# Input tiles spread over all partitions and loaded at once, at the head of a fused Fourier and two-layer kernel

## The chip, the core and the metric

The kernel runs on one core of a Trainium2 chip. The metric is device time in microseconds (us). The five engines are TensorE (PE, matmuls; its weight loads are PEld), VectorE (DVE), ScalarE (ACT), GpSimd (POOL) and SyncE (SP). DMAs are issued from queues of SP, ACT or POOL and are carried by 16 DMA engines. SBUF is the on-chip memory of 128 partitions, PSUM holds the results of matmuls.

## What is computed

The input x has two batches of 3008 tokens with 256 values. A Fourier stage mixes tokens, two dense layers follow:

```
X = np.fft.rfft(x, axis=1)
Yr = Xr @ w_r - Xi @ w_i + b_r
Yi = Xr @ w_i + Xi @ w_r + b_i
Y = soft threshold of Yr, Yi by 0.01
x = np.fft.irfft(Y, n=3008, axis=1)
h = x @ w_in;  x = (h * clip(h + 3, 0, 6) / 6) @ w_out
x = (silu(x @ w_gate) * (x @ w_val)) @ w_out2
```

## The kernel before

The transform of length 3008 = 47 x 64 is done in two stages. The first one (`pre(n)`, lines L239 to L254) takes a tile of x: 94 rows (two sets of 47, padded to QP = 96) on the partitions and 1024 columns. It multiplies it with the table `fwd1_sb` (two matmuls of 512 columns, four records in the trace, at L245), evicts the halves on ACT (L248) and DVE (L250) into a buffer `bs` of a ring of four, and writes it to a DRAM scratch `Bd` from ACT's queue (L252). That DMA is kept back in `out_b` and issued in the next tile's `pre`, after its copies. Each batch has NT = 8 tiles; tiles 0 to 7 are the first batch, 8 to 15 the second.

The second stage works on groups Q of four frequencies. `load_q` loads a table `m` (L270) and `z`, the transposed view of Bd (L279); it needs all eight writes of the batch. `s2` (S in the order below, L287 to L294) does the second transform, in two halves, with evictions on ACT and DVE and a split into a high and a low part, `xh` and `xl`. `ln` (L) mixes with the complex weights `linh`, `linl` in three passes at L113, L114 and L115, thresholds on DVE, and `ia` (A, L333) begins the way back. After that units of the dense layers follow, to the end of the kernel.

The loads: `load_x(n)` (L213) puts tile n into one of four buffers of the ring `xal`/`xah`, which are needed later by the dense layer under the same names. Three tiles are loaded ahead, then `pre(n)` loads tile n + 3, and waits on SP until the buffer is free. The mixing weights (`lin_st`), the bias and `inv2_sb`, a table for the last transform, are loaded from POOL's queue, in `prepare` (L228), and POOL splits the weights into high and low parts. Three matmuls on zeros (L225) run before the first tile arrives.

The order of the work is written out by hand in the list `seq` (L366): tile 0, `prepare`, tiles 1 to 7, the load of the first group, tiles 8 to 10, S(0); then, for each group, L, A, S of the next group, and two of the tiles that are left (`rest`) while there are any. `pre_conv` also steps the conversion of the dense layer's weights (`conv1`: loads `st` at L151, small steps on ACT and DVE) from tile 9 on. DMA semaphores are eight and are used in turn, so that a DMA can also wait for an earlier one that raised the same semaphore.

Of the kernel before, what the change touches and what calls it, by code (L numbers as in the profile page):

```python
# [24 lines left out]
QP = 96  # L25
# [15 lines left out]
def dft_tables():  # L41


    tp = 2 * np.pi
    n1 = np.arange(N1)
    f = np.zeros((N1, NG, 2))
    for g in range(NG):
        a = tp * ((n1 * g) % N1) / N1
        f[:, g, 0], f[:, g, 1] = np.cos(a), -np.sin(a) * (g > 0)
    fwd1 = np.zeros((2, N1, NG, 2, 2))  # L50
    for q in range(2):
        fwd1[q, :, :, q, :] = f
    fwd1 = np.pad(fwd1.reshape(QN, GW), ((0, QP - QN), (0, 0)))
    fwd2 = np.zeros((NG, 2, 2, NJ, 2, K2))
    inv1 = np.zeros((NG, 2, K2, 2, 2, NJ))
    for g in range(NG):
        k = g + N1 * np.arange(K2)
        own = np.ones(K2) if g else (np.arange(K2) <= K2 // 2) * 1.0
        edge = (k == 0) | (k == SEQ // 2)
        sg = np.where(k > SEQ // 2, -1.0, 1.0)  # L60
        w = np.where(edge, 1.0, 2.0) / SEQ
        for q in range(2):
            a = tp * (np.outer(2 * np.arange(NJ) + q, k) % SEQ) / SEQ
            c, sn = np.cos(a) * own, np.where(edge, 0.0, np.sin(a)) * own
            ci = np.where(edge, 0.0, c)
            fwd2[g, q, 0, :, 0], fwd2[g, q, 0, :, 1] = c, -sn * sg
            inv1[g, 0, :, q, 0], inv1[g, 1, :, q, 0] = (w * c).T, -(w * sn * sg).T
            if g:
                fwd2[g, q, 1, :, 0], fwd2[g, q, 1, :, 1] = sn, c * sg
                inv1[g, 0, :, q, 1], inv1[g, 1, :, q, 1] = (w * sn).T, (w * ci * sg).T  # L70
    fwd2 = fwd2.reshape(NG, 128, 128).transpose(1, 0, 2).reshape(128, NG * 128)
    inv1 = inv1.reshape(NG, 128, 128).transpose(1, 0, 2).reshape(128, NG * 128)
    out = {"fwd1": fwd1, "inv2": fwd1.T, "fwd2": fwd2, "inv1": inv1}
    return {n: np.ascontiguousarray(v, dtype=np.float32) for n, v in out.items()}


# [1 line left out]
def fourier_moe_kernel(ctx: ExitStack, tc: tile.TileContext, x, lin, bias, w1, w2, fwd1, inv2, fwd2,  # L78
# [39 lines left out]
        nc.vector.tensor_tensor(out=o, in0=full, in1=hi.bitcast(F32), op=ALU.subtract)  # L118

    misc = pool(ctx, "misc", "left")  # L120
    fwd1_sb = misc.tile([QP, GW], F32, name="fwd1_sb")
    inv2_sb = misc.tile([GW, QP], F32, name="inv2_sb")

    three = misc.tile([128, 32], F32, name="three")[:, :1]
# [87 lines left out]

    def load_x(n):  # L213
        b, i = divmod(n, NT)
        if b < NB:
            xt[n] = xs_p.tile([128, 4 * DIM], F32, tag="xah" if n % 2 else "xal", name=f"x{b}_{i}", bufs=2)
            nc.sync.dma_start(xt[n][:QP], x[b][:, i * 4 * DIM : (i + 1) * 4 * DIM])

    nc.sync.dma_start(fwd1_sb, fwd1)
    for n in range(3):  # L220
        load_x(n)

    p = psf[0]([128, 512], "p0")
    for n in range(3):
        nc.tensor.matmul(p, zeros[:, :128], zeros, start=True, stop=True)  # L225
    conv1 = pieces(w1p, "w1", w1, KF1, 2, W1)

    def prepare():  # L228
        lin_st = ap_.tile([128, 2, 2, DIM], F32, tag="z", name="lin_st", bufs=3)
        nc.gpsimd.dma_start(lin_st, lin)  # L230
        nc.gpsimd.dma_start(bias_sb, bias)
        nc.gpsimd.dma_start(inv2_sb, inv2)
        for dh in range(2):
            for k in range(2):
                hi, lo, st = linh[:, dh, k], linl[:, dh, k], lin_st[:, dh, k]
                nc.gpsimd.tensor_copy(hi, st)
                nc.gpsimd.tensor_tensor(out=lo, in0=st, in1=hi.bitcast(F32), op=ALU.subtract)

    def pre(n):  # L239
        b, i = divmod(n, NT)  # L240
        load_x(n + 3)
        bs = ring4(f"bs{b}_{i}")
        for h in range(2):
            p = psf[0]([GW, 512], f"p1_{b}_{i}_{h}")
            nc.tensor.matmul(p, fwd1_sb, xt[n][:QP, h * 512 : (h + 1) * 512], start=True, stop=True)  # L245
            o = bs[:GW, h * 512 : (h + 1) * 512]
            if h == 0:
                nc.scalar.copy(o, p)  # L248
            else:
                nc.vector.tensor_copy(o, p)  # L250
        sent()
        out_b.append(lambda: nc.scalar.dma_start(Bd[b][:, i * 4 * DIM : (i + 1) * 4 * DIM], bs[:GW]))  # L252
        if i == NT - 1:
            sent()  # L254
# [554 lines left out]
```

## Time and profile before

| what | us |
|---|---|
| median of 3 runs (1246.06 to 1247.27) | 1246.06 |
| profiled execution | 1247.67 |
| its span | 1245.9 |
| PE busy | 1228.3 |
| DVE busy | 809.8 |
| ACT busy | 679.7 |

The span is the time from the first to the last instruction in the profiled execution, and times below count from its start. A chain of waits is followed back from the last instruction; each piece of it is either work or the landing of a DMA that released the next piece. The time of a DMA is told from its issue to its landing.

### The profile page before, as it was taken

To read this page: it belongs to the slowest core of one execution; us is meant where nothing else is said; L and a number is where in the kernel's file an instruction comes from. 1 tells how busy PE (TensorE), PEld (TensorE's weight loads), DVE (VectorE), ACT (ScalarE), POOL (GpSimd) and SP (SyncE) were. 2 spreads that over 40 slices of the span, in tenths; PEclk is the share of its full clock that TensorE was granted. 3 is DMA by queue.
4 is the path that set the end of the run, shared out by engine and by line. 5 is a ranking of instruction groups with operands and counts; after the bars stand their busy time and mean duration, and the time that the engine had idled before them with its cause. 6 is when DMAs were issued, how large, how long until landed. Compare 5 with 4: busy or idle time off the path is not lost.

```text
span 1245.9 us, 15942 instructions
## 1 busy us (share of the span) xinstructions
PE 1228.3 (99%) x5914; PEld 1034.2 (83%) x5914; DVE 809.8 (65%) x1424; ACT 679.7 (55%) x1216; POOL 6.3 (1%) x15
## 2 busy tenths in 40 slices
PE   7899999999999999999999999999999999999998
PEld 2799987888888888888899888888888888888997
DVE  2587665666666666666656577676676676676665
ACT  2455544555555555555555566656656555656554
POOL 2000000000000000000000000000000000000000
PEclk9899999999999999999999999999999999999999
DMA  9976323033122122132032244554644644544551
GB/s 305 279 258 191 102 77 105 28 100 103 64 91 93 59 70 93 64 100 91 39 105 91 72 175 170 203 182 152 220 158 170 235 153 152 216 157 168 203 186 72
DMA packets 50285, 172.84 MB, mean 139 GB/s; under 512 B 4752, under 2 KB 18160, under 8 KB 39456
## 3 DMA queue, kind: packets, MB, share of 16 engines
q1 hardware_dynamic: 41856, 158.55, 37.4%
q10 hardware_dynamic: 8128, 12.58, 2.8%
q8 instruction: 46, 0.75, 0.2%
q0 software_dynamic: 224, 0.69, 0.2%
q14 instruction: 31, 0.25, 0.1%
HBM read 132.75 MB, written 39.06 MB: 138 GB/s over the span
## 4 chain that ended last, share of the span: by engine, by line
PE 96%; DMA 2%; DVE 0%; ACT 0%; issue 0%; SPq 0%; ACTq 0%; DVEq 0%
PE acc L114 12%; PE acc L115 12%; PE acc L113 12%; PE ph L113 7%; PE ph L115 7%; PE ph L114 7%; PE P L662 5%; PE P L663 5%; PE P L664 5%; PE Tb L663 3%; PE Tb L662 3%; PE Tb L664 3%; PE p L419 3%; PE p L113 2%; PE p L115 2%; PE p L114 2%
## 5 line engine op out<-in xcount | busy, mean ns | idle before, releaser
L434 DVE SCALAR_TENSOR_TENSOR r<-r,ph 128x512 f32<-128x512 f32 (+1 forms) x192 | 129.7, 676 | 83.3 <-ACT r L433 82.8
L118 DVE TENSOR_TENSOR gl<-r,gh 128x512 fp32r<-128x512 f32 (+1 forms) x192 | 130.1, 678 | 82.4 <-ACT gh L452 81.0
L433 ACT ACTIVATE r<-ph,three 128x512 f32<-128x512 f32 (+1 forms) x192 | 130.2, 678 | 96.1 <-PE ph L115 80.6
L452 ACT CAST gh<-r 128x512 fp32r<-128x512 f32 (+1 forms) x192 | 117.3, 611 | 84.4 <-DVE r L434 82.7
L113 PE MATMUL ph<-xah,w1l 128*128 128x512 f32 (+1 forms) x384 | 152.1, 396 | 0.0
L113 PE MATMUL acc<-gh,w1l 128*128 128x512 f32 (+1 forms) x384 | 148.3, 386 | 1.5 <-ACT gh L452 1.5
L114 PE MATMUL acc<-gl,w1h 128*128 128x512 f32 (+1 forms) x384 | 148.2, 386 | 0.2 <-DVE gl L118 0.2
L115 PE MATMUL ph<-xah,w1h 128*128 128x512 f32 (+1 forms) x384 | 148.2, 386 | 0.0
L114 PE MATMUL ph<-xal,w1h 128*128 128x512 f32 (+1 forms) x384 | 148.1, 386 | 0.0
L115 PE MATMUL acc<-gh,w1h 128*128 128x512 f32 (+1 forms) x384 | 148.1, 386 | 0.0
L118 DVE TENSOR_TENSOR gl<-s,gh 128x512 fp32r<-128x512 f32 (+1 forms) x144 | 97.3, 676 | 49.8 <-ACT gh L686 49.7
L662 PE MATMUL P<-xo,slot 128*128 128x512 f32 (+1 forms) x288 | 111.3, 386 | 1.7 <-DVE g L732 0.8
L114 PE MATMUL acc<-gl,slot 128*128 128x512 f32 (+1 forms) x288 | 111.1, 386 | 0.3 <-DVE gl L118 0.2
L113 PE MATMUL acc<-gh,slot 128*128 128x512 f32 (+1 forms) x288 | 111.0, 385 | 0.0
L664 PE MATMUL P<-xo,slot 128*128 128x512 f32 (+1 forms) x288 | 110.9, 385 | 0.0
L115 PE MATMUL acc<-gh,slot 128*128 128x512 f32 (+1 forms) x288 | 110.9, 385 | 0.0
L663 PE MATMUL P<-xo,slot 128*128 128x512 f32 (+1 forms) x288 | 110.9, 385 | 0.0
L728 ACT ACTIVATE s<-g 128x512 f32<-128x512 f32 (+1 forms) x72 | 44.9, 623 | 93.7 <-DVE g L726 93.7
L686 ACT CAST gh<-s 128x512 fp32r<-128x512 f32 (+1 forms) x144 | 88.1, 612 | 1.5 <-DVE s L745 1.2
L113 PEld LDWEIGHTS acc<-gh,w1l 128*128 128x128 f32 x384 | 72.1, 188 | 15.4 <-ACT gh L452 1.9
L114 PEld LDWEIGHTS acc<-gl,w1h 128*128 128x128 f32 x384 | 72.1, 188 | 14.6 <-DVE gl L118 0.9
L115 PEld LDWEIGHTS ph<-xah,w1h 128*128 128x128 f32 x384 | 72.1, 188 | 14.0
(94 smaller groups left out, 2258.7 us busy)
## 6 DMA issues: line engine op xcount, KB each, us to landing
slot<-Wd SPq DMA_DIRECT2D x72, 1152.0 KB, 5.1
st<-in_w SPq DMA_DIRECT2D x68, 256.0 KB, 3.8
Wd<-slot SPq DMA_DIRECT2D x12, 1152.0 KB, 4.7
x<-in_x SPq DMA_DIRECT2D x16, 384.0 KB, 6.5
Bd<-bs ACTq DMA_DIRECT2D x16, 384.0 KB, 5.9
z<-Bd SPq DMA_DIRECT2D x12, 512.0 KB, 6.1
Cd<-cs ACTq DMA_DIRECT2D x12, 512.0 KB, 3.5
Xd<-x SPq DMA_DIRECT2D x20, 256.0 KB, 2.1
```

What stands on the lines that cost most here:

```text
L113: nc.tensor.matmul(o, wl, xh, start=start, stop=False)
L114: nc.tensor.matmul(o, wh, xl, start=False, stop=False)
L115: nc.tensor.matmul(o, wh, xh, start=False, stop=stop)
L118: nc.vector.tensor_tensor(out=o, in0=full, in1=hi.bitcast(F32), op=ALU.subtract)
L433: nc.scalar.activation(r[:, :n], p[:, :n], AF.Relu, bias=three)
L434: nc.vector.scalar_tensor_tensor(out=r[:, :n], in0=r[:, :n], scalar=6.0, in1=p[:, :n], op0=ALU.min, op1=ALU.mult)
L452: nc.scalar.copy(hi[:, :n], g[:, :n])
L662: nc.tensor.matmul(o, wl, x[:, 0, :n], start=start, stop=False, skip_group_check=not start)
L663: nc.tensor.matmul(o, wh, x[:, 1, :n], start=False, stop=False, skip_group_check=not start)
L664: nc.tensor.matmul(o, wh, x[:, 0, :n], start=False, stop=True, skip_group_check=not start)
L686: nc.scalar.copy(hi[:, :nb], t[:, :nb])
L728: nc.scalar.activation(s0[:, :n], h, AF.Silu)
```

## The change

- `fwd1_sb` becomes 128 x 192. Its first 96 columns are the old table in the first 96 rows. In the second 96 columns the first 64 rows of the table lie on the even partitions, the last 32 on partitions 1, 5, 9 and so on, and the other partitions are zero.
- A tile of x can come in two forms: as before on partitions 0 to 95 (tiles 0, 1, 8, 9, 12, 13), or spread in the same pattern over all 128 partitions, by two DMAs (the others). For the spread form six buffers are filled with zeros once, three by DVE and three by POOL, and their matmuls contract over 128 partitions.
- The input lies in DRAM tile by tile now; it was row by row.
- The first batch has eight buffers: the four of the ring and four that the attention stage uses later (`xl`, `xh`). All eight tiles are issued at the start, with `lin_st` and the bias, now from SP's queue, between tiles 4 and 5. Tiles 8 to 11 are issued in `pre(1)` to `pre(4)`, 12 to 15 in `pre(9)` to `pre(12)`.
- Two matmuls on zeros instead of three. `prepare` is only POOL's splitting, and `inv2_sb` is loaded at group NQ of the loop, from SP.
- Four tiles of the second batch (8 to 11) run before S(0), and tile 12 between S(0) and the first L. Three are left for the loop instead of five. The conversion is stepped from tile 11 on.

```diff
-    out = {"fwd1": fwd1, "inv2": fwd1.T, "fwd2": fwd2, "inv1": inv1}
+    both = np.zeros((128, 2 * GW))
+    both[:QP, :GW] = fwd1
+    both[::2, GW:], both[1::4, GW:] = fwd1[:64], fwd1[64:]
...
-        if b < NB:
-            xt[n] = xs_p.tile([128, 4 * DIM], F32, tag="xah" if n % 2 else "xal", name=f"x{b}_{i}", bufs=2)
-            nc.sync.dma_start(xt[n][:QP], x[b][:, i * 4 * DIM : (i + 1) * 4 * DIM])
+        t = xt[n] = room[n if n < NT else n % 4][:, : 4 * DIM]
+        if n % 4 < 2 and not 4 <= n < NT:
+            nc.sync.dma_start(t[:QP], x[b, i])
+        else:
+            nc.sync.dma_start(t[::2], x[b, i, :64])
+            nc.sync.dma_start(t[1::4], x[b, i, 64:])
...
+        if n > 1:
+            (nc.gpsimd if n % 2 else nc.vector).memset(t[:, : 4 * DIM], 0.0)
+    for n in range(5):
         load_x(n)
+    lin_st = ap_.tile([128, 2, 2, DIM], F32, tag="z", name="lin_st", bufs=3)
+    nc.sync.dma_start(lin_st, lin)
+    nc.sync.dma_start(bias_sb, bias)
+    for n in range(5, NT):
+        load_x(n)
...
-    for n in range(3):
+    for n in range(2):
         nc.tensor.matmul(p, zeros[:, :128], zeros, start=True, stop=True)
...
-        load_x(n + 3)
+        if 1 <= n <= 4:
+            load_x(n + 7)
+        elif 9 <= n <= 12:
+            load_x(n + 3)
...
-        if n > NT:
+        if n > NT + 2:
             conv1.step()
...
-    seq = P[:1] + [prepare] + P[1:NT] + [lambda: load_q(0, 0)] + P[NT : NT + 3] + S(0)
-    rest = P[NT + 3 :]
+    seq = [prepare] + P[:NT] + [lambda: load_q(0, 0)] + P[NT : NT + 4] + S(0) + P[NT + 4 : NT + 5]
+    rest = P[NT + 5 :]
...
-            seq += [lambda: load_ct(blocks[0])]
+            seq += [lambda: nc.sync.dma_start(inv2_sb, inv2), lambda: load_ct(blocks[0])]
```

SP's queue at the head of the program, before: the loads of tiles 4 to 7 of batch one and tiles 0 to 2 of batch two (`x0_` and `x1_`), then the table and z of the first group. `DMAHW` are the DMA semaphores, `PE` is a wait for matmuls.

```order
L217 DMA x0_4_171<-in_x 96x1024 [waits DMAHW1_49,PE_49]
L217 DMA x0_5_181<-in_x 96x1024 [waits DMAHW2_49,PE_49]
L217 DMA x0_6_191<-in_x 96x1024 [waits DMAHW3_49,DMAHW0_49,PE_49]
L217 DMA x0_7_201<-in_x 96x1024 [waits DMAHW4_49,PE_49]
L217 DMA x1_0_211<-in_x 96x1024 [waits DMAHW5_49,PE_49]
L217 DMA x1_1_221<-in_x 96x1024 [waits DMAHW7_49,DMAHW6_49,PE_49]
L217 DMA x1_2_231<-in_x 96x1024 [waits DMAHW0_49,PE_49]
L270 DMA m0_242<-in_fwd2 128x512 [waits DMAHW2_49]
```

The same queue now, from tile 4 to tile 7 of batch one (`room4` to `room7`, two DMAs each).

```order
L222 DMA room4_114<-in_x 64x1024 [waits DMAHW0_49,DVE_49]
L223 DMA room4_114<-in_x 32x1024 [waits DMAHW2_49]
L238 DMA lin_st_130<-in_lin 128x1024 [waits DMAHW3_49]
L239 DMA bias_sb_106<-in_bias 128x256 [waits DMAHW5_49]
L222 DMA room5_116<-in_x 64x1024 [waits DMAHW6_49,Pool_49]
L223 DMA room5_116<-in_x 32x1024 [waits DMAHW0_49]
L222 DMA room6_118<-in_x 64x1024 [waits DMAHW1_49,DVE_49]
L223 DMA room6_118<-in_x 32x1024 [waits DMAHW2_49]
L222 DMA room7_120<-in_x 64x1024 [waits DMAHW3_49,Pool_49]
L223 DMA room7_120<-in_x 32x1024 [waits DMAHW5_49]
```

No wait for PE is left there, but semaphores are. ACT's rows of now tell which DMA two of them belong to: the copy into `bs0_4`, which has the buffer of `bs0_0`, waits for the first write of Bd by DMAHW6, and the copy into `bs0_5` for the second by DMAHW1. The loads of `room5` and `room6` wait for the same two.

```order
L274 DMA Bd0_60<-bs0_0_182 96x1024 [waits DVE_49,Activation_49]
L270 COPY bs0_2_199<-p1_0_2_0_200 96x512 [waits PE_49]
L274 DMA Bd0_60<-bs0_1_190 96x1024 [waits DMAHW1_49,DVE_49,Activation_49]
L270 COPY bs0_3_209<-p1_0_3_0_210 96x512 [waits PE_49]
L274 DMA Bd0_60<-bs0_2_199 96x1024 [waits DMAHW4_49,DVE_49,Activation_49]
L270 COPY bs0_4_219<-p1_0_4_0_220 96x512 [waits DMAHW6_49,PE_49]
L274 DMA Bd0_60<-bs0_3_209 96x1024 [waits DMAHW7_49,DVE_49,Activation_49]
L270 COPY bs0_5_227<-p1_0_5_0_228 96x512 [waits DMAHW1_49,PE_49]
```

The writes follow the copies of the next tile, as they did. On PE around S(0), before: the last tile of batch two ahead of it (`p1_1_2`), S(0) itself (`p2_0_0`), and the first mixing matmuls (`p3_0_0`).

```order
L245 MATMUL p1_1_2_0_270<-x1_2_231,fwd1_sb_82 96x512 [waits DMAHW0_49,Activation_49]
L245 MATMUL p1_1_2_1_273<-x1_2_231,fwd1_sb_82 96x512 [waits DVE_49]
L287 MATMUL p2_0_0_0_285<-m0_242,z0_0_244 128x128 [waits DMAHW6_49,DMAHW2_49,DVE_49]
L287 MATMUL p2_0_0_0_285<-m0_242,z0_0_244 128x128 x3
L287 MATMUL p2_0_0_1_294<-m0_242,z0_0_244 128x128 [waits Activation_49]
L287 MATMUL p2_0_0_1_294<-m0_242,z0_0_244 128x128 x3
L113 MATMUL p3_0_0_0_309<-linh_104,xl_0_0_284 128x256 [waits DVE_49,Pool_49]
```

PE at the same place now.

```order
L267 MATMUL p1_1_3_0_284<-room3_112,fwd1_sb_82 96x512 [waits DMAHW7_49,DMAHW5_49,Activation_49]
L267 MATMUL p1_1_3_1_287<-room3_112,fwd1_sb_82 96x512 [waits DVE_49]
L309 MATMUL p2_0_0_0_299<-m0_252,z0_0_254 128x128 [waits DMAHW2_49,DMAHW0_49,Activation_49]
L309 MATMUL p2_0_0_0_299<-m0_252,z0_0_254 128x128 x3
L309 MATMUL p2_0_0_1_308<-m0_252,z0_0_254 128x128 [waits DVE_49]
L309 MATMUL p2_0_0_1_308<-m0_252,z0_0_254 128x128 x3
L265 MATMUL p1_1_4_0_320<-room0_108,fwd1_sb_82 96x512 [waits DMAHW3_49,Activation_49]
L265 MATMUL p1_1_4_1_323<-room0_108,fwd1_sb_82 96x512 [waits DVE_49]
L116 MATMUL p3_0_0_0_335<-linh_104,xl_0_0_298 128x256 [waits DVE_49,Pool_49]
```

Tile 11 (`p1_1_3`) has moved ahead of S(0), and tile 12 (`p1_1_4`) between it and the mixing.

## Rows read from the trace of the kernel before

**Rows 1.** The page, engines: busy us, share of the span, instructions.

```profile
PE 1228.3 (99%) x5914; PEld 1034.2 (83%) x5914; DVE 809.8 (65%) x1424; ACT 679.7 (55%) x1216; POOL 6.3 (1%) x15
```

**Rows 2.** Chain of waits, 0 to 45 us: start, us, what.

```profile
1.66 7.00 DMA x<-in_x
...
22.30 6.03 DMA Bd<-bs
...
28.45 5.74 DMA z<-Bd
...
34.33 2.06 PE p L287 x8
...
40.09 0.36 PE p L113
...
42.56 1.72 PE p L245 x4
44.28 1.79 PE p L287 x16
```

**Rows 3.** Timeline, PE, first 30 us: start, us, instruction, [idle before <- releaser].

```profile
1.48 4.80 PE L225 MATMUL p<-zeros 128*128 128x512 f32 x6 [1.48 <-DVE zeros L127]
...
6.12 1.88 PE L245 MATMUL p<-x,fwd_sb 96*96 96x512 f32 x4
...
8.70 12.75 PE L245 MATMUL p<-x,fwd_sb 96*96 96x512 f32 x28 [0.70 <-DMA x<-in_x]
...
24.23 3.75 PE L245 MATMUL p<-x,fwd_sb 96*96 96x512 f32 x8 [0.61 <-DMA x<-in_x]
```

**Rows 4.** DMA view, 2 to 11 us, then 11 to 28: packets, MB, share.

```profile
DMA packets 757, 2.44 MB, mean 271 GB/s; under 512 B 158, under 2 KB 158, under 8 KB 757
q1 hardware_dynamic: 533, 1.75, 71.9%
...
DMA packets 1827, 6.17 MB, mean 363 GB/s; under 512 B 257, under 2 KB 257, under 8 KB 1827
q1 hardware_dynamic: 890, 2.86, 51.6%
q10 hardware_dynamic: 937, 3.31, 50.6%
```

**Rows 5.** DMA view, issues at 1.20, 9.90, 22.30, 28.45, 28.95, 34.21: us to landing.

```profile
x<-in_x SPq DMA_DIRECT2D x1, 384.0 KB, 4.0
...
Bd<-bs ACTq DMA_DIRECT2D x1, 384.0 KB, 4.1
...
Bd<-bs ACTq DMA_DIRECT2D x1, 384.0 KB, 6.0
...
z<-Bd SPq DMA_DIRECT2D x1, 512.0 KB, 5.7
...
x<-in_x SPq DMA_DIRECT2D x1, 384.0 KB, 7.0
...
z<-Bd SPq DMA_DIRECT2D x1, 512.0 KB, 8.5
```

**Rows 6.** Timeline, ACT's queue: the first write of Bd.

```profile
9.90 0.36 ACTq L252 DMA_DIRECT2D Bd<-bs  x1
```

**Rows 7.** Windows, A:B length, busy of PE, PEld, DVE, ACT, POOL, PEclk, DMA.

```profile
32.00:33.00 1.00, 0.00 (x0) 0.00 (x0) 0.00 (x0) 0.00 (x0) 0.00 (x0) 0.89 0.94 255
...
39.00:40.00 1.00, 0.75 (x4) 0.48 (x3) 0.69 (x1) 0.24 (x2) 0.00 (x0) 0.70 1.02 331
...
60.00:1240.00 1180.00, 1176.53 (x5706) 1003.28 (x5704) 784.68 (x1376) 658.78 (x1173) 0.00 (x0) 1.00 0.38 131
```

**Rows 8.** Timeline: DVE's fill with zeros, and issues of SP.

```profile
0.94 0.48 DVE L127 MEMSET zeros<- 128x512 f32 x1
...
19.80 1.02 SPq L270 DMA_DIRECT2D m<-in_fwd  x1
```

More of the change, by code (lines that the diff above doesn't have):

```diff
@@ L72, in dft_tables @@
     inv1 = inv1.reshape(NG, 128, 128).transpose(1, 0, 2).reshape(128, NG * 128)
-    out = {"fwd1": fwd1, "inv2": fwd1.T, "fwd2": fwd2, "inv1": inv1}
+    both = np.zeros((128, 2 * GW))
+    both[:QP, :GW] = fwd1
+    both[::2, GW:], both[1::4, GW:] = fwd1[:64], fwd1[64:]
+    out = {"fwd1": both, "inv2": fwd1.T, "fwd2": fwd2, "inv1": inv1}
     return {n: np.ascontiguousarray(v, dtype=np.float32) for n, v in out.items()}
@@ L120, in fourier_moe_kernel @@
     misc = pool(ctx, "misc", "left")
-    fwd1_sb = misc.tile([QP, GW], F32, name="fwd1_sb")
+    fwd1_sb = misc.tile([128, 2 * GW], F32, name="fwd1_sb")
     inv2_sb = misc.tile([GW, QP], F32, name="inv2_sb")
@@ L214, in load_x @@
         b, i = divmod(n, NT)
-        if b < NB:
-            xt[n] = xs_p.tile([128, 4 * DIM], F32, tag="xah" if n % 2 else "xal", name=f"x{b}_{i}", bufs=2)
-            nc.sync.dma_start(xt[n][:QP], x[b][:, i * 4 * DIM : (i + 1) * 4 * DIM])
-    nc.sync.dma_start(fwd1_sb, fwd1)
-    for n in range(3):
+        t = xt[n] = room[n if n < NT else n % 4][:, : 4 * DIM]
[4 more added lines that the diff above has]
+            nc.sync.dma_start(t[1::4], x[b, i, 64:])
+    nc.sync.dma_start(fwd1_sb, fwd1)
+    room = []
+    for n in range(NT):
+        if n < 4:
+            t = xs_p.tile([128, 4 * DIM], F32, tag="xah" if n % 2 else "xal", name=f"room{n}", bufs=2)
+        else:
+            t = ap_.tile([128, 6 * DIM], F32, tag="xh" if n % 2 else "xl", name=f"room{n}", bufs=2)
+        room.append(t)
+        if n > 1:
[6 more added lines that the diff above has]
+    for n in range(5, NT):
         load_x(n)
     p = psf[0]([128, 512], "p0")
-    for n in range(3):
+    for n in range(2):
         nc.tensor.matmul(p, zeros[:, :128], zeros, start=True, stop=True)
@@ L228, in prepare @@
     def prepare():
[L229 to L232, printed above, removed]
         for dh in range(2):
@@ L244, in pre @@
             p = psf[0]([GW, 512], f"p1_{b}_{i}_{h}")
-            nc.tensor.matmul(p, fwd1_sb, xt[n][:QP, h * 512 : (h + 1) * 512], start=True, stop=True)
+            if n % 4 < 2 and not 4 <= n < NT:
+                nc.tensor.matmul(p, fwd1_sb[:QP, :GW], xt[n][:QP, h * 512 : (h + 1) * 512], start=True, stop=True)
+            else:
+                nc.tensor.matmul(p, fwd1_sb[:, GW:], xt[n][:, h * 512 : (h + 1) * 512], start=True, stop=True)
             o = bs[:GW, h * 512 : (h + 1) * 512]
@@ L771 @@
     xp = x.reshape(NB, N1, NJ, 2, DIM).transpose(0, 3, 1, 2, 4).reshape(NB, QN, NJ * DIM)
-    xp = np.pad(xp, ((0, 0), (0, QP - QN), (0, 0)))
+    xp = np.pad(xp, ((0, 0), (0, QP - QN), (0, 0))).reshape(NB, QP, NJ // 4, 4 * DIM).transpose(0, 2, 1, 3)
     bias = np.repeat(np.stack([b_r, b_i]), 64, axis=0)
```

## The prediction

> **What bounds the kernel now.** I read the page first, for the engines' shares: PE is busy for 99% of the span [rows 1]. Then the windows: from 60 to 1240 us PE is busy for 1176.5 of 1180 us [rows 7], so nothing in that stretch can be shortened by loading earlier, and the change leaves the number of matmuls there as it is, except for tiles that it moves out. What is left is the first 40 us, and there the chain of waits tells the order [rows 2]: a load of x to 8.66, 13 us of first-transform matmuls (L245) and an eviction, the last write of the first batch into Bd (22.30 to 28.33), the load of z from it (28.45 to 34.19), the second transform (L287) at 34.33, and the first mixing matmul after which PE never pauses again at 40.09. The end of the kernel is this point plus the PE work that is then left. So the change is worth: how much earlier S(0), the second transform of group 0, can begin (34.33 now), what PE does beside it, and how many tiles are already behind it.
>
> [...] First, DMA: from 2 to 11 us, where nearly only loads run, the engines move 271 GB/s; from 11 to 28 us, with as many writes as loads, 363, and they are full in both [rows 4]. By queue (bytes over share of the window): the SP queue, which has the loads, 1.75 MB/(0.719 x 9 us) = 270 GB/s and 2.86/(0.516 x 17) = 326; the ACT queue, the writes of Bd, 3.31/(0.506 x 17) = 385. A load into a block of 96 partitions thus holds the engines 1.2 to 1.4 times as long as a write of the same bytes. Second, PE: 28 matmul records (7 tiles of four) take 12.75 us from 8.70 [rows 3], 1.82 us a tile against 1.72 where nothing is late [rows 2]. The first stage is almost PE's own pace, with 0.7 us of holes. [...]
>
> **The first tiles.** The warm-up loses one of three matmuls: six records took 4.80 us [rows 3], so PE is free 1.6 us earlier, at 4.7. The first tile lands at 1.20 + 4.0 = 5.2 [rows 5], and PE began it at 6.12 [rows 3]: 0.9 us won. The second landed at 8.66 behind `lin`; now it is ahead of it, so tile 1 follows at 6.9. The three zero fills on DVE are 128x1024: twice 0.48 us each [rows 8], done by 4.3 us, before DVE's first eviction. POOL's three fills have no row near them; tile 3's load waits for the first, and at a due time of 10.3 and 4.0 for a load it has until 6 us. Each split tile needs two issues of SP, at most 1.0 us each [rows 8]; seven issues end by 8 us, and only at that price would tile 3 be late, by 2 us, which the wait of tile 5 below covers.
>
> **All eight tiles at once: less than it says.** The built program's waits (in the section on the change) show that DMA semaphores are used in turn: tile 5's first DMA waits for the one that the first write of Bd raises, tile 6's for the second write's, tile 11's last for the sixth's. The first write was issued 1.2 us after tile 1's matmuls began (8.70 to 9.90, [rows 3, 6]) and landed after 4.1 [rows 5]. Now: 6.9 + 1.2 + 4.1 = 12.2; plus 4.0 for the shortest load [rows 5], tile 5 is there at 16.2. It was begun at 8.70 + 4 x 1.82 = 16.0. Tile 6: second write at 8.6 + 1.2 = 9.8, landed at 13.9, load there at 18.0; tile 7 is issued right behind, so PE is done with it at 18.0 + 2 x 1.72 = 21.4, against 21.45 now. So the gain of 2 us at tiles 0 to 4 is given back by tile 7, unless a load lands sooner than the 4.0 that I know. The eviction and the eighth write then start at 22.3 as they do now.
>
> **What the eighth write meets.** It took 6.0 us, the first one 4.1 [rows 5]: the difference is the loads of batch two beside it. Afterwards the loads of tiles 8 to 11 are issued at about 16 to 19 us, and six of the first eight tiles and tiles 10 and 11 are spread over all partitions. If a spread load runs at the 385 GB/s of the writes instead of 270 to 326, eight tiles of 0.39 MB save 8 x 0.18 to 8 x 0.43 = 1.5 to 3.5 us of engine time; about 1 us is lost while the SP queue stands before tile 5. Bounds for the write: 4.1 to 6.0 us. I take 4.2, near the quiet row, because most of the queue ahead has gone by 24 us; the write lands at 26.5 instead of 28.33. z then takes 5.7 [rows 5] (the next z took 8.5 in a fuller queue, which is the bad end): S(0) at 32.4, **1.9 us earlier**, with a range of 2 us later to 4 us earlier.
>
> **Tiles 11 and 12.** Tile 11 now runs while PE waits for z: 1.72 us [rows 2] leave the path for good, covered by an idle time that was 6.35 us (27.98 to 34.33). If tile 11's load were late, S(0) would wait behind it, PE being in order; its last part is issued after the sixth write's landing at about 24, so it lands near 28 and ends by 30. Tile 12 stands between S(0) and the mixing matmuls. It doesn't leave the path, but fills a hole. Its own load follows z in the queue; the load behind z, issued at 28.95, took 7.0 [rows 5] and so came 1.8 us after z; S(0) covers 1.8.
>
> **Clock and hole.** From 34.33 to 40.09 PE did 1.79 us of L287 and six mixing matmuls (6 x 0.12) at full-clock prices, 2.5 of 5.76 us: 3.3 lost. [...] If it stays up, the mixing matmul of 40.09, which waits for the second half's low part, can go at S(0) + 4.75 (5.76 less the 1.0 that S(0)'s first half gains), and PE has 1.79 + 1.72 + 0.7 = 4.2 to do till then: 0.55 lost. **Gain 2.75.** If it falls as before, 5.3 us at half speed cost 2.65, and the gain is 0.6.
>
> **At nothing:** two steps of the weight conversion come later (DVE and ACT have room in the 60 to 1240 us stretch, and the units force the conversion on); `inv2` is loaded late, long before its first use; the splitting of `lin` on GpSimd starts after about 11 us and is needed at 35; the second z is issued when the first lands, as now, and its 8.5 us fit in the 8.6 that S(0), tile 12, half a mixing group and tile 13 take, with no slack: up to 1 us could be lost there.
>
> **Sum.** 1.9 + 1.7 + 2.75 = 6.35 us. The profiled execution took 1247.67 us (span 1245.9, 1.8 around it), so 1241.3; the median of the runs, 1246.06, lies 1.6 lower: **1239.7**.
>
> **The rivals.** [...] (B) *Loads still wait for writes*: the spread form brings no rate (the two windows differ for another reason), and the eighth write lands at 28.3 as before or up to 1.5 us later. With the clock falling, 1.7 + 0.6 = 2.3 and less: 1244.5. For it speaks that tile 7 is no earlier in my own sum, against it the 385 of the writes. (C) *The pairs land one after the other*: each split tile pays the 4.0 us of a load twice. On the path are tiles 5, 6 and 7, 3 x 4.0 = 12 us later, S(0) at 44.4; with 1.7 and 0.6 back that is 10.1 - 2.3 = 7.8 slower: 1254. It turns slower by more than 0.2% from 2.2 us a tile on. Against it: seven tiles were worked off 1.82 us apart [rows 3], so loads one behind the other land no further apart than that. [...]
>
> **How the numbers follow.** The forecast 0.47 (its own range 1237.6 to 1241.6, from S(0) 4 us to no time earlier), A 0.26, B 0.18, C 0.09. A measurement can tell about 0.2%, 2.5 us, so faster means below 1243.6. Forecast and nearly all of A, and a little of B: faster 0.74; the rest of A and B: same 0.17; C: slower 0.09. The range, 1237.5 to 1245.0, holds the forecast but its best corner, A, and most of B.
>
> **What would show it.** Right: the x loads alone above 330 GB/s before 10 us; a hole of 1 to 3 us in L245's matmuls at tile 5; S(0) near 32.4; no slice of lower clock between 30 and 40 us; PE without holes from about 36. Wrong: tiles 5 to 7 without a hole (then S(0) is earlier and I am too careful), a lower clock after z (A), the eighth write past 28 us (B), PE holes at the second z, or load landings of 8 us at tiles 5 to 7 (C).

## The result, and the profile after

The changed kernel takes **1263.80 us** (median of four runs, 1260.44 to 1264.75), the kernel before 1246.66 beside it: 1.0132 times as long, with a 95% interval of 1.0112 to 1.0152. The forecast was 1239.7, with a range up to 1245.0. It was wrong by 24 us, and in sign.

The page of the kernel after (span; engines with busy us, share, instructions), which answers [rows 1]:

```profile
span 1262.0 us, 15953 instructions
PE 1241.7 (98%) x5912; PEld 1034.4 (82%) x5912; DVE 812.4 (64%) x1427; ACT 679.4 (54%) x1216; POOL 7.2 (1%) x15
```

PE is busy for 13.4 us more, with two instructions fewer. So most of the loss is no idle time: the same matmuls take longer. Equal windows of time show where. Kernel after; columns are the window, its length, the busy time of PE, PEld, DVE, ACT and POOL with the number of instructions, the granted clock, the DMA share and GB/s:

```profile
2.00:11.00 9.00, 8.72 (x18) 3.03 (x17) 4.17 (x6) 1.76 (x4) 1.46 (x2) 1.00 1.00 305
11.00:28.00 17.00, 12.69 (x27) 4.50 (x26) 4.33 (x7) 3.25 (x6) 4.31 (x8) 0.90 0.92 310
...
240.00:640.00 400.00, 400.00 (x1828) 328.24 (x1827) 249.82 (x465) 209.94 (x349) 0.00 (x0) 1.00 0.23 75
722.00:785.00 63.00, 62.22 (x273) 50.90 (x272) 43.35 (x67) 39.05 (x67) 0.00 (x0) 1.00 0.51 188
790.00:900.00 110.00, 110.00 (x477) 89.27 (x477) 74.06 (x116) 63.47 (x110) 0.00 (x0) 1.00 0.48 173
```

The same places of the kernel before (layer 2 began 11 us earlier there):

```profile
240.00:640.00 400.00, 400.00 (x1874) 336.05 (x1874) 255.58 (x475) 215.15 (x359) 0.00 (x0) 1.00 0.24 79
712.00:775.00 63.00, 62.22 (x274) 50.88 (x273) 44.36 (x69) 38.41 (x67) 0.00 (x0) 1.00 0.50 184
780.00:890.00 110.00, 110.00 (x487) 91.10 (x486) 75.52 (x117) 64.48 (x112) 0.00 (x0) 1.00 0.48 173
```

In layer 1 (240 to 640 us) PE has no idle time in either kernel, at a granted clock of 1.00 of full speed, but it does 1874 matmuls in 400 us before and 1828 after: **2.5% fewer in the same time**. The first pair of token blocks of layer 2 (712 to 775) is as fast as it was (274 and 273), the second (780 to 890) does 477 instead of 487. Following the same matmul through both traces, the kernel after is late by 2.1 us at 120 us (the start), by 11.2 at the first matmul of layer 2, by 2.2 more after the second pair and 2.2 more after the fourth, and by 15.9 at the end. The stretch that the prediction had set aside (60 to 1240 us) has lost six times as much as the stretch it worked out.

The start itself, timeline of PE in the kernel after (start, us, instruction, [idle before <- releaser]); it answers [rows 3]:

```profile
1.48 3.37 PE L245 MATMUL p<-zeros 128*128 128x512 f32 x4 [1.48 <-DVE zeros L130]
5.13 3.65 PE L265 MATMUL p<-room,fwd_sb 96*96 96x512 f32 x8 [0.28 <-DMA room<-in_x]
8.61 5.31 PE L267 MATMUL p<-room,fwd_sb 128*96 128x512 f32 x12
18.23 6.92 PE L267 MATMUL p<-room,fwd_sb 128*96 128x512 f32 x12 [4.31 <-DMA room<-in_x]
24.99 3.60 PE L265 MATMUL p<-room,fwd_sb 96*96 96x512 f32 x8
28.43 1.88 PE L267 MATMUL p<-room,fwd_sb 128*96 128x512 f32 x4
32.56 1.93 PE L267 MATMUL p<-room,fwd_sb 128*96 128x512 f32 x4 [2.25 <-DMA room<-in_x]
37.76 3.13 PE L309 MATMUL p<-m,z 128*128 128x128 f32 x16 [3.27 <-DMA z<-Bd]
```

Tiles 0 to 4 are worked off early and without a hole, until 13.9 us. Then PE stands 4.3 us for tile 5, does tiles 5 to 7 in 6.92 us (part of it at half the clock), waits for tile 11, and begins S(0) at 37.76 instead of 34.33. Part of this is given back behind S(0); from 70 us on the kernel is 2.1 us late. After both of the longer waits (4.31 and 3.27 us) the granted clock was lower, 0.50 and 0.51 of full speed (third number from the end):

```profile
18.00:21.40 3.40, 3.17 (x4) 1.23 (x5) 0.00 (x0) 0.58 (x1) 0.00 (x0) 0.50 0.87 270
38.40:41.90 3.50, 3.50 (x15) 2.85 (x14) 0.69 (x1) 1.88 (x5) 0.00 (x0) 0.51 1.01 358
```

### The profile page after: what moved, and what is told of

Its sections match the earlier page's. It is cut to its first block, busy times and chain, and to the rows that moved or that the text cites. A ratio compares the mean times of both kernels' runs of the same rounds, so it can differ in the third digit from the quotient of the medians.

```text
span 1262.0 us, 15953 instructions
## 1 busy us (share of the span) xinstructions
PE 1241.7 (98%) x5912; PEld 1034.4 (82%) x5912; DVE 812.4 (64%) x1427; ACT 679.4 (54%) x1216; POOL 7.2 (1%) x15
## 4 chain that ended last, share of the span: by engine, by line
PE 94%; DMA 4%; DVE 1%; ACT 1%; issue 0%; POOL 0%; SPq 0%; ACTq 0%; DVEq 0%
PE acc L117 12%; PE acc L118 12%; PE acc L116 12%; PE ph L116 7%; PE ph L118 7%; PE ph L117 7%; PE P L684 5%; PE P L686 5%; PE P L685 5%; PE Tb L686 3%; PE Tb L684 3%; PE Tb L685 3%; PE p L441 3%; PE p L116 2%; PE p L118 2%; PE p L117 2%
## 5 line engine op out<-in xcount | busy, mean ns | idle before, releaser
L118 PEld LDWEIGHTS acc<-gh,w1h 128*128 128x128 f32 x384 | 72.3, 188 | 15.1
```

What stands on the lines that cost most here:

```text
L118: nc.tensor.matmul(o, wh, xh, start=False, stop=stop)
```

## The experiments: where the 14 us went

What had moved in the long stretch, if no instruction had? The widened table is the first tile of the first pool on the left side of SBUF, so everything behind it on that side now stands 384 bytes further on in each partition: the operands xah, xal, gh, gl, slot and half of xo. The tiles on the right side (W1, the other half of xo) did not move. In layer 1 every matmul with the weights W1 takes one operand from the left and one from the right; in layer 2 so do those of xo in every second pair of token blocks, the one whose xo lies on the right. Theory: the rate depends on how the two operands stand to each other in SBUF. Rivals: the new loading causes it all; or the place of the left tiles causes it by itself. The right side can be moved alone too, by the constant EDGE, the bytes of an unused tile at its end.

**p1: the wide table alone, on the kernel before.**

```diff
-    fwd1_sb = misc.tile([QP, GW], F32, name="fwd1_sb")
+    fwd1_sb = misc.tile([QP, 2 * GW], F32, name="fwd1_sb")[:, :GW]
```

> The kernel before with one edit: the tile of the first table is 192 columns wide instead of 96, and only its first 96 columns are used, so that everything behind it on the left side of SBUF stands 384 bytes further on and nothing else changes. Theory 'placement' (the matmuls between 230 and 1250 us are slower because their operands stand elsewhere in SBUF; the profile of after has 232 ns instead of 227 from one 512-column matmul's start to the next in layer 1 and in every second pair of token blocks of layer 2): about 1246.7 + 13.8 = 1260.5 us, with the first 120 us as before. Rival 'loads' (all 16 us come from the new loading at the start and what it displaces later): 1246.7 us, no change.

Measured: 1261.59 us against 1247.17, ratio 1.0126 (1.0107 to 1.0144). An edit that touches no instruction costs 14.4 us.

**p2: the changed kernel, right side moved by the same 384 bytes.**

```diff
-EDGE = 480
+EDGE = 96
```

> The changed kernel with the right side of SBUF moved by the same 384 bytes (EDGE 96 instead of 480), so that left and right tiles stand to each other as before. If what counts is how left and right tiles stand to each other: 1263.8 - 13.8 = 1250 us, of which about 2 to 3 us above the kernel before are the loading at the start. If what counts is where the left tiles stand by themselves: still 1264 us. If placement has no part: 1264 us.

Measured: 1249.34 us, ratio to before 1.0018 (1.0009 to 1.0027). The 14 us are back, with the left tiles where the change had put them, so their place by itself is not it.

**p3: the kernel before, right side moved alone (EDGE 480 to 864).**

> The kernel before with the right side of SBUF moved the other way by 384 bytes (EDGE 864 instead of 480), the left side where it was: left and right then stand to each other as in the changed kernel, while no left tile has moved. If the relation of the two sides counts: about 1260.5 us, slow in the same places (layer 1, every second pair of blocks in layer 2). If the place of the left tiles by itself counts: 1246.7 us.

Measured: 1262.73 us, 1.0124 (1.0109 to 1.0139), the same loss without moving one left tile.

**p4: the changed kernel with a filler, left side at 1024 bytes from its old place.**

```diff
+    misc.tile([128, 160], F32, name="fill")
     three = misc.tile([128, 32], F32, name="three")[:, :1]
```

> The changed kernel with 640 bytes of filler behind the widened table, so that the left tiles stand 1024 bytes further on than in the kernel before (multiples of 1024 again) and the right side is where it was. If only the offset within 1024 bytes counts, by the relation of the sides or by the left tiles alone: 1250 us. If any distance other than that of before costs: 1260 us or more.

Measured: 1249.53 us, 1.0016 (1.0007 to 1.0025). The window 240 to 640 us of p2, p3 and p4, in this order, each from its own trace:

```profile
240.00:640.00 400.00, 400.00 (x1873) 335.76 (x1873) 255.45 (x474) 215.89 (x360) 0.00 (x0) 1.00 0.24 78
```
```profile
240.00:640.00 400.00, 400.00 (x1828) 328.35 (x1828) 250.01 (x465) 209.88 (x349) 0.00 (x0) 1.00 0.23 75
```
```profile
240.00:640.00 400.00, 400.00 (x1874) 336.04 (x1874) 255.56 (x474) 215.18 (x359) 0.00 (x0) 1.00 0.24 80
```

The number of matmuls alone tells which kernel has the old relation of the two sides.

**m1: the disputed cost by itself.** Groups of 32 equal matmuls, from group to group only the weights' place changes:

```python
CASES = [(0, 64 * k) for k in range(32)]   # bytes: moving operand, weights
...
for n in range(32):
    nc.tensor.matmul(p, ws[:, w // 4 : w // 4 + 128], xs[:, m // 4 : m // 4 + 512], start=True, stop=True)
```

> Does none of the computation: it only times TensorE. 64 warm-up matmuls, then 45 groups of 32 identical matmuls of 512 columns (fp32r, as in the dense layers), each with its own weight load, with ScalarE and VectorE idle. From group to group only the distance in bytes between the weights and the moving operand in SBUF changes: 0 to 1984 in steps of 64, then the same distances with the moving operand moved too, then some small ones. Theory 'TensorE's own two reads collide': groups at distances 0, 512, 1024 and 1536 take 32 x 227 ns = 7.25 us, those at 128 and 384 beyond a multiple of 512 take 32 x 232 ns = 7.43 us or more, and the moved pairs go by their distance alone. Rival 'it takes the reads and writes of ScalarE and VectorE beside it': all groups take 7.25 us.

Timeline of PE (start, us, instruction); the last letter counts the steps of 64 bytes, a is 0 (the operands are fp32r, the type of the dense layers' operands; the trace prints f32):

```profile
20.49 7.41 PE L111 MATMUL ataa<-xs,ws 128*128 128x512 f32 x32
27.75 7.63 PE L111 MATMUL atab<-xs,ws 128*128 128x512 f32 x32
35.21 7.60 PE L111 MATMUL atac<-xs,ws 128*128 128x512 f32 x32
42.65 7.49 PE L111 MATMUL atad<-xs,ws 128*128 128x512 f32 x32
49.98 7.44 PE L111 MATMUL atae<-xs,ws 128*128 128x512 f32 x32
57.25 7.63 PE L111 MATMUL ataf<-xs,ws 128*128 128x512 f32 x32
```

From one group's start to the next, divided by 32: 226.9 ns at a distance of 0 bytes, 233.1 at 64, 232.5 at 128, 229.1 at 192, and 227.2 again at 256. The pattern repeats up to 1984 bytes. With the moving operand moved too, the distance alone counts (moving at 384: 227 ns with weights at 384, 896 and 1408, 232.8 with weights at 512); 8 bytes cost 4 ns, 16 to 48 bytes 6 to 7. Behind the warm-up m1's program has instructions for TensorE alone, and the group at a distance of 64 takes 7.63 us at 27.75 us, the one at 1856 (64 beyond a multiple of 256) the same 7.63 at 234.29; so other engines' work does not make the difference. In the changed kernel the weight loads (188 ns each) overlap the matmuls: they are busy for 82% of its span, the matmuls for 98%. That the two disturb each other by their addresses is my reading of m1; no row shows it. My expectation had 512 as the period; it is half of that. By m1 the two operands of layer 1 stand a multiple of 256 apart in the kernel before (227 ns from one start to the next) and 128 beyond one in the changed kernel, since 384 is 256 + 128, and its 2.5% are m1's 232.5 to 226.9, 5.6 ns per matmul.

In the slow pairs of layer 2 the distance of a matmul's own operands is not the whole account. The `acc` matmuls there take gh or gl and slot, which all lie on the left and have kept their distance. Still they are as slow as the xo matmuls around them; the kernel after, in the second pair:

```profile
853.41 0.40 PE L116 MATMUL acc<-gh,slot 128*128 128x512 f32 x1
853.64 0.40 PE L117 MATMUL acc<-gl,slot 128*128 128x512 f32 x1
853.88 0.40 PE L118 MATMUL acc<-gh,slot 128*128 128x512 f32 x1
854.11 0.39 PE L116 MATMUL acc<-gh,slot 128*128 128x512 f32 x1
854.34 0.39 PE L117 MATMUL acc<-gl,slot 128*128 128x512 f32 x1
854.57 0.40 PE L118 MATMUL acc<-gh,slot 128*128 128x512 f32 x1
854.80 0.40 PE L684 MATMUL P<-xo,slot 128*128 128x512 f32 x1
```

Over the whole pair they start 232.0 ns apart and the xo matmuls 232.3, against 226.7 for both in the kernel before; p1 shows the same 232.0 and 232.3. Slowing the xo matmuls alone by 5.6 ns would cost 252 x 5.6 ns = 1.4 us a pair, and 2.2 were measured. In m1 all matmuls of a group are equal, so it can't tell whether a matmul slows its neighbours too; this was not tested.

**p5 and p6: does m1's rule predict the kernel?** The kernel before with EDGE 736 (256 bytes) and EDGE 544 (64 bytes).

> The kernel before with the right side of SBUF moved by 256 bytes (EDGE 736). The stand-alone matmuls repeat with a distance of 256 bytes (7.26, 7.46, 7.44, 7.33 us for 32 matmuls at 0, 64, 128, 192 bytes beyond a multiple of 256). If this rule holds in the kernel: no change, 1247.2 us. If any move from the chosen place costs: 1255 us or more.

> The kernel before with the right side of SBUF moved by 64 bytes (EDGE 544). In layer 1 the weights stand on the right, at 192 bytes beyond a multiple of 256 from the moving operand: 2.2 ns more per matmul instead of the changed kernel's 5.75, so 9.4 x 2.2 / 5.75 = 3.6 us. In the odd pairs of blocks of layer 2 the moving operand stands on the right, so the weights are at 64 bytes: 6.25 ns more, 4.5 x 6.25 / 5.75 = 4.9 us. Sum 8.5 us: 1255.7 us. If the sign of the distance doesn't count, 5 us (1252.4) or 15 us (1262).

Measured: p5 1246.99 us, 0.9999 (0.9990 to 1.0009), no change, as the rule has it. p6 1254.07 us against 1247.18, 1.0057 (1.0044 to 1.0071): 6.9 us where I had 8.5, and clearly neither 5 nor 15. Its two windows (layer 1, then the second pair of layer 2):

```profile
240.00:640.00 400.00, 400.00 (x1859) 333.21 (x1858) 253.42 (x470) 213.75 (x355) 0.00 (x0) 1.00 0.24 78
780.00:890.00 110.00, 110.00 (x477) 89.21 (x476) 74.12 (x116) 63.12 (x111) 0.00 (x0) 1.00 0.47 172
```

Layer 2 pays as much as in the changed kernel (477 there too), layer 1 a third of what it paid there (15 matmuls fewer than 1874, against 46): the sign counts, as weights and moving operand stand on opposite sides in the two layers. One thing did not fit: by the starts of the same matmuls layer 1 lost 1.3 us in the end, where I had 3.6. It had lost 3.4 by 630 us, near what was foretold, and won part of it back in its last two token blocks, which are 448 columns wide. The matmuls of these blocks started 200.1 ns apart on the mean in p6, holes left aside, and 205.8 in the kernel before (most of them 206 or 207). The last run asks whether a width of 448 has another best distance.

**c1: b2 (below), and the narrow blocks of layer 1 moved by 64 bytes inside their tiles.**

```diff
+    def cut(n):
+        o = 0 if n == BLK else 16
+        return slice(o, o + n)
...
-            mm3(p[:, :n], wh[w], wl[w], xh[:, dh, :n], xl[:, dh, :n], dh == 0, dh == 1)
+            mm3(p[:, :n], wh[w], wl[w], xh[:, dh, cut(n)], xl[:, dh, cut(n)], dh == 0, dh == 1)
```

> b2 with one more edit: in layer 1's last two token blocks, which are 448 columns wide, the moving operands (xah, xal, gh, gl) start 64 bytes further on in their tiles, so that the weights stand at 192 beyond a multiple of 256 from them; everything 512 columns wide stays at a multiple of 256. In p6 the 448-column matmuls of layer 1 stood at 192 and started 200.0 ns apart (655 to 700 us: 225 of layer 1), against 206.7 in the kernel before at 0. If that was the distance and the narrow matmuls have an order of their own: 384 x 6.7 ns = 2.6 us under b2 (1246.0 against 1247.2 for the kernel before), so 1243.5 to 1244.5 us, and 227 matmuls instead of 220 in a window of 45 us there. If p6's narrow blocks were quicker for another reason (the right side's absolute place, other engines): no change to b2, 220 matmuls.

Measured: **1244.65 us** against 1246.95, ratio 0.9983 (0.9974 to 0.9992), the one version whose interval lies below the kernel before, by 2.3 us or 0.2%. The window of the narrow blocks, in c1 and then in b2:

```profile
655.00:700.00 45.00, 45.00 (x227) 42.18 (x226) 29.12 (x48) 25.55 (x44) 0.00 (x0) 1.00 0.17 64
```
```profile
655.00:700.00 45.00, 45.00 (x220) 40.86 (x219) 28.75 (x47) 24.64 (x42) 0.00 (x0) 1.00 0.17 63
```

227 and 220, as foretold, and 200.1 ns from start to start on the mean, 205.7 in b2. The gain within layer 1 is 2.0 us against b2 (profiled executions) where I had 2.6: the 206.7 of the expectation leaves out the shorter spacings. So the distance counts at 448 columns too, but there 192 bytes beyond a multiple of 256 is better than 0, and so is 128 (203.9 ns in the changed kernel, whose narrow blocks gained a little). Which distance is best at other widths, and for layer 2's narrow blocks, was not measured.

## The experiments: the start

With its placement mended the changed kernel (p4) is still about 2 us slower than the kernel before, where 6 us less were forecast. The queues show what stood in the way; the rows are those of the changed kernel itself (in p4's profile the two longest of these waits are 6.7 and 3.9 us). Waits of SP's queue up to 80 us (line, waited for: us in total, times, longest):

```profile
SPq L222 <- DMA Bd<-bs: 7.5, 2, 4.4
SPq L223 <- DMA Bd<-bs: 7.1, 1, 7.1
```

and from the timeline of the queues (first piece of tile 5's load, the second DMA of tile 11, z, and on ACT the eighth write as the second of two):

```profile
12.74 0.48 SPq L222 DMA_DIRECT2D room<-in_x  x1
...
28.50 0.47 SPq L223 DMA_DIRECT2D room<-in_x  x1
...
30.40 0.40 SPq L301 DMA_DIRECT2D z<-Bd  x1
```
```profile
24.41 3.20 ACTq L274 DMA_DIRECT2D Bd<-bs  x2
```

L222 and L223 are the two DMAs of a spread tile. They wait for writes of Bd because semaphores are used in turn, as foreseen; not foreseen was that tile 11's would stand 7.1 us, and that the eighth write would stand nearly 3 us on ACT, until 27.3, for the landing of the fifth (issued at 20.34, landed 6.9 us later). Five variants of p4 undo parts of the change, and two variants of the kernel before have one part alone.

**h1: block form for every tile.** One DMA per tile on 96 partitions, no zero rows:

```diff
-        if n % 4 < 2 and not 4 <= n < NT:
-            nc.sync.dma_start(t[:QP], x[b, i])
-        else:
-            nc.sync.dma_start(t[::2], x[b, i, :64])
-            nc.sync.dma_start(t[1::4], x[b, i, 64:])
+        nc.sync.dma_start(t[:QP], x[b, i])
```

> On the changed kernel with its old placement relation restored (640 bytes of filler, as in p4): every input tile in block form, on 96 partitions with one DMA, no zero rows; the eight buffers, the loads at once and the new order stay. Fewer DMAs mean that no load of the first batch waits for a write of a result. Theory 'the pairs of DMAs cost the start': tile 5 begins at 15 to 16 us instead of 18.2, S(0) at 33 to 35 instead of 37.8, whole time 1 to 3 us under p4, 1246 to 1249 us. Rival 'it is loading at once that costs': S(0) at 37 to 38 as in after, 1249.5 us.

**h2: the mixing weights back on POOL's queue.**

```diff
-    nc.sync.dma_start(lin_st, lin)
-    nc.sync.dma_start(bias_sb, bias)
     def prepare():
+        nc.gpsimd.dma_start(lin_st, lin)
+        nc.gpsimd.dma_start(bias_sb, bias)
```

> On p4 again: the spread tiles stay, but the mixing weights and their bias go over POOL's queue as in the kernel before, so that tiles 5 to 7 stand on SP right behind tile 4. Theory 'tile 5 is late since its DMAs stand behind the mixing weights and then behind the first write': tile 5 begins at 14 to 16 us, S(0) at 35 to 36, 1247 to 1249 us. Rival 'spread loads are late whatever stands ahead of them': S(0) at 37 to 38 us, 1249.5 us.

**h3: the new order alone, on the kernel before** (with it the conversion's steps from tile 11 on).

```diff
-... + P[NT : NT + 3] + S(0)
+... + P[NT : NT + 4] + S(0) + P[NT + 4 : NT + 5]
```

> The kernel before with the new order alone: four tiles of batch two ahead of S(0), tile 12 right behind it, and the conversion's steps from tile 11 on. Loads, tables and placement as before. If the order alone brings what the prediction had for it (about 1.7 us less idle time ahead of S(0), given back where the tile stood): 1246 to 1247 us, S(0) at 34.3 us as before. If tile 11 and the later loads push z's DMA back: S(0) at 35 to 36 us, 1247 to 1249 us.

**h6: the old order back, on p4** (with it the conversion's steps from tile 9 on).

> On p4 (the changed kernel with its placement restored, 1249.5 us): the old order back (three tiles of batch two ahead of S(0), the conversion's steps from tile 9 on); spread tiles, eight buffers and the mixing weights on SP stay. If the order costs the 1.5 us that it cost by itself on the kernel before: 1248 us. If the order is neutral where the loads run ahead: 1249.5 us.

**h4: only the conversion's steps back (`n > NT`), on p4.**

> On p4: only the conversion's first two steps back to tiles 9 and 10. If the late first piece of the weights (its DMA stands behind the loads of tile 15, and ScalarE waits 3.8 us for it ahead of S(1)'s casts) costs time: 1247.5 to 1248.5 us and no idle time of TensorE around 55 us. If earlier steps put two more DMAs ahead of z's: 1249.5 to 1251 us.

**h5: h1 and h2 together.**

> On p4: both undone, block form for every tile and the mixing weights over POOL's queue; eight buffers at once and the new order stay. Each alone brought the time back to that of the kernel before (1246.9 and 1247.5 us). If they mend the same loss (tile 5's late DMA): 1246 to 1248 us. If their gains add: 1244 to 1245 us.

**b1: eight buffers alone, on the kernel before** (block form, old order, narrow table, mixing weights on POOL). What hangs on them comes along: two matmuls on zeros, inv2_sb loaded late, x tile by tile in DRAM.

> The kernel before with one part of the change: eight buffers, so that the first batch is loaded at once, in block form; old order, narrow table (so placement as before), mixing weights on POOL. If TensorE's waits for tiles 0 to 7 are what the early part is worth: 2 to 3 us under the kernel before, 1244.5 us. If the early part is bound by what the DMA engines move ahead of z (they are 90% busy from 4 us on), loading tiles sooner changes nothing: 1246.5 to 1247.5 us.

Measured, the ratio of each against executions of the kernel before beside it; the S(0) column and the windows come from one profiled execution of each:

| kernel | us | ratio (95%) | S(0) at | GB/s 2 to 11 | GB/s 11 to 28 |
|---|---|---|---|---|---|
| before | 1247.2 to 1247.6 | 1 | 34.3 | 271 | 363 |
| p4 | 1249.53 | 1.0016 (1.0007 to 1.0025) | 37.8 | 308 | 307 |
| h1 block form | 1246.89 | 0.9991 (0.9982 to 1.0001) | 36.1 | 283 | 367 |
| h2 weights on POOL | 1247.49 | 0.9998 (0.9989 to 1.0008) | 36.5 | 320 | 320 |
| h3 order alone | 1249.06 | 1.0012 (1.0003 to 1.0022) | 40.0 | 276 | 350 |
| h6 old order | 1251.90 | 1.0034 (1.0022 to 1.0046) | 37.3 | 302 | 321 |
| h4 conversion | 1248.96 | 1.0016 (1.0007 to 1.0025) | 37.6 | 318 | 314 |
| h5 both | 1247.51 | 0.9999 (0.9990 to 1.0007) | 36.8 | 277 | 363 |
| b1 eight buffers | 1249.37 | 1.0016 (1.0007 to 1.0025) | 34.8 | 279 | 363 |

h1 and h2 each take the loss away, and together no more than one alone, as if they mended the same thing; nothing is left of a gain. In h1 and h5 the DMA engines move no less than before in either window. h2 did not go as I had it: tile 5 follows tile 4 at once, but the hole moves to tile 6 (3.1 us at 19.6), so the spread loads are late there too. And h2 has the time of the kernel before with 320 GB/s from 11 to 28 us instead of 363, so the lower rate by itself does not cost the 2 us; which of the waits does is not shown. h4 was to remove two holes of the mixing matmuls after 55 us in the changed kernel's profile (0.42 and 0.86 us). They are gone, but p4's profile has neither of them already, and h4's has one of 0.90 us at 44.4; the time did not follow by more than can be told. Order and loading depend on each other: by itself the new order costs about 1.5 us (tile 11 waits 6.45 us for its load, and S(0) behind it), while in p4 taking it back costs about 2.2 (1.0034 against 1.0016). b1 says most: with all eight loads running ahead and the old order, tiles 0 to 7 do not bring S(0) forward (34.8 against 34.3). Loading earlier is worth nothing here; its expectation had put that down to the DMA engines, which move the same 363 GB/s from 11 to 28 us as before. That b1 is 2 us slower was not expected, and why was not settled.

**m2 and m3: the rate of loads by their form.** Eight tile loads in groups, in block and in spread form, without and with eight writes of the same size beside them.

```python
for spread in (False, True):
    for writes in (False, True):
        for n in range(NT):            # 8 loads, block or spread, and the writes if any
            ...
        nc.vector.tensor_copy(mark, room[:, :, 0])   # ends when all eight have landed
```

> Does none of the computation: it times transfers alone. Three times over, four groups of eight tile loads (384 KB each, into one buffer each): block form, block form with eight writes of 384 KB from 96 partitions to DRAM over ScalarE's queue at the same time, spread form (two DMAs per tile), spread form with the same writes; a copy by VectorE of one column of all tiles ends each group. From the windows of the whole kernels (2 to 11 us, loads alone: 271 to 283 GB/s in block form, 305 to 320 spread; 11 to 28 us, loads and writes: 363 to 367 in block form, 310 to 320 spread): if the form of the loads makes that difference, the rates here are about 275, 365, 310 and 315 GB/s. If the waits for semaphores made it, spread with writes is no slower here than block form with writes.

In m2 the writes were not tied to their groups and ran ahead into all of the first four, so its rates say little. m3 holds each group until the one before has ended.

> As m2, in which the writes ran ahead of their groups on ScalarE's queue, with each group's transfers held until the group before has ended, writes included. 8 loads are 3.15 MB, 8 writes as much. In m2 eight loads without writes took 13.9 to 15.0 us in block form and 13.1 to 13.4 spread, and beside the stray writes 20 us in block form and 28.5 spread. If spread loads lose the contest with writes: eight loads alone 14 us in block form and 13 us spread; with eight writes the loads end after 16 to 20 us in block form and 2 us or more later when spread, though all 6.3 MB take about as long. If m2's 28.5 us came from the writes of the groups before: both forms end at about the same time.

Timeline of VectorE in m3 (start, us, instruction, [idle before <- releaser]): block alone, block with writes, spread alone, spread with writes, and block alone again. The idle time in brackets is the group's time in all rows but the third; the third group's first loads went out at 44.43, its bracket begins later.

```profile
25.37 0.17 DVE L114 COPY mark<-room 128x8 f32<-128x8 f32 x1 [14.36 <-DMA room<-in_x]
...
44.23 0.17 DVE L114 COPY mark<-room 128x8 f32<-128x8 f32 x1 [18.68 <-DMA room<-in_x]
...
57.82 0.17 DVE L114 COPY mark<-room 128x8 f32<-128x8 f32 x1 [12.34 <-DMA room<-in_x]
...
80.36 0.17 DVE L114 COPY mark<-room 128x8 f32<-128x8 f32 x1 [22.35 <-DMA room<-in_x]
...
94.91 0.17 DVE L114 COPY mark<-room 128x8 f32<-128x8 f32 x1 [14.37 <-DMA room<-in_x]
```

Alone, eight tiles take 14.3 us in block form and 13.4 spread (44.4 to 57.8): 7% less. Beside writes they take 18.7 us in block form and **22.4** spread, 3.7 more, and the windows of these two groups, writes included, show 317 and 282 GB/s:

```profile
25.57:45.41 19.84, 0.17 (x1) 0.59 (x3) 0.00 (x0) 1.00 0.87 317
...
58.02:80.36 22.34, 0.01 (x1) 0.39 (x2) 0.00 (x0) 1.00 0.85 282
```

Three repetitions agree within 0.8 us (block with writes 18.7, 18.9, 19.4; spread with writes 22.4, 22.2, 22.3). There is next to no waiting for a write's semaphore in m3 (2.8 us in the whole run), so it is the rate. What slows the spread loads there was not settled: the two DMAs per tile, or the step over the partitions.

**b2: the version that follows**, h5 with only tiles 2 and 3 spread, whose loads land before the first write.

> The version the runs point to: placement restored, eight buffers at once, the new order, the mixing weights over POOL, and only tiles 2 and 3 spread, whose loads land ahead of the first write; everything behind them in block form. If spread loads are faster alone and slower beside writes: 1245.5 to 1247 us, under h5's 1247.5. If two tiles are too few to matter: 1247.5 us.

Measured: 1246.01 us against 1247.18, ratio of the means 0.9997 (0.9987 to 1.0007): the rates are there (317 GB/s from 2 to 11 us, 360 after), and the time is that of the kernel before. By the start alone no version tried is faster than it by what can be measured; c1 is, by layer 1.

## Where the prediction went wrong

- *From 60 to 1240 us nothing changes, since the number of matmuls stays.* **This step failed**, and it made 14 of the 24 us (p1: 14.4; after less p4: 14.3). The prediction saw that no work moved there, and took "same matmuls" for "same time"; the runs showed 232 instead of 227 ns from one of layer 1's matmuls to the next. The edit that did it was not among the parts that it costed: the table's width, which moved the operands by 384 bytes.
- *First tiles.* Right: tile 0 at 5.13 (5.2 foretold), tiles 0 to 4 done at 13.9 without a hole.
- *Tile 5 waits for the first write's semaphore.* Right in kind: its first DMA was issued at 12.74 (12.2 foretold). Too small in size: its second went at 13.26 and took 4.7 us, tile 5 began at 18.23 instead of 16.2, and the 4.3 us hole was followed by a lower clock (0.50 granted from 18.0 to 21.4 us), which I had only looked for after z. Tile 7 was done at 25.2, not 21.4.
- *The eighth write, issued at 22.3, lands at 26.5.* The landing time was mis-sized in my disfavour (3.0 us, 4.2 taken), the issue was missed: it stood on ACT until 27.3, behind the late tiles and then behind the fifth write's semaphore. I had followed the reuse of semaphores for the loads, not for the writes. z took 7.2 us instead of 5.7. So S(0) came 3.4 us later than before, beyond even the 2 us that the prediction allowed.
- *Spread loads run at the 385 GB/s of writes.* **Failed.** Alone the rate rose from 271 to 305 (I wanted over 330), and between 11 and 28 us it fell from 363 [rows 4] to 310. I had derived the gain from a window in which loads and writes ran together, and m3 shows that there the spread form is the slower one.
- *Tile 11 leaves the path, 1.72 us.* Not by itself: its second DMA waited 7.1 us and it ended at 34.5, in front of S(0) (h3 shows the same on the kernel before, 6.45 us).
- *Clock and hole, 2.75 us.* It went as in A, the case in which the clock falls, only earlier and twice: low at 18 to 21 us (0.50) and again around S(0) (0.72 from 38 to 39, 0.50 from 39 to 41), 3.13 us for sixteen records. No run shows that the clock stays up when PE stands still for 3.4 us, on which the 2.75 rested: ahead of this S(0) PE had stood for 3.27, and in h2 for 3.63, with 3.04 us for the sixteen records.
- *Rivals.* B (loads wait for writes, no rate) is nearest to the start as it was; it had 1244.5, and p4, the change without its placement, measured 1249.5: B too kept the gain of tile 11, and had the eighth write land at most 1.5 us later than before, where in the changed kernel it landed at 30.3 instead of 28.3. C did not happen: tiles 5 to 7 ran without a hole between them.

The sum of 6.35 us had three terms, and all rested on the loads coming sooner. Of the whole miss of 24 us, 14 are placement and about 9 (2.3 slower where 6.4 faster stood) the start; the last one is the kernel before itself, at 1247.2 in most runs where the sum began from 1246.06. Which of the waits makes the start 2 us slower stays open.

## What to carry to other kernels

An edit that changes a tile's size moves the tiles behind it (here by 384 bytes); print the addresses of the matmuls' operands before and after, and measure the matmul's rate at a few distances of weights and moving operand for its own width (of the distances measured, a multiple of 256 bytes was best at 512 columns, 192 beyond one at 448). To find such a loss, count an engine's instructions in equal windows in which it is busy throughout: 1874 against 1828 says it at once, where busy shares say 100% twice. And where the DMA engines are full (in b1 a share of 0.99 from 2 to 11 us and 1.01 from 11 to 28), ask first what loads and writes together get: eight loads issued sooner brought S(0) no earlier there (34.8 against 34.3).

## What the hardware showed that I had not expected

- The rate of 512-column fp32r matmuls depends on the distance between weights and moving operand modulo 256 bytes: 226.9 ns at 0, 233.1 at 64, 232.5 at 128, 229.1 at 192 (m1), in the kernel up to 14.4 us of 1247 (p1). At 448 columns it is 205.7 ns on the mean at 0 (b2) and 200.1 at 192 (c1). In layer 2 matmuls whose own operands kept their distance slowed down with their neighbours, 232.0 ns instead of 226.7 (p1).
- Loads spread over all 128 partitions took 13.4 us for eight tiles instead of 14.3 alone, and 22.4 instead of 18.7 beside writes (m3).
